# Batch 0 of an attention and mixer kernel: keys ahead of queries, U and V loaded later, the shifted keys in two steps

## The chip, the cores and the metric

The kernel runs on one core of one Trainium2 chip. The metric is the device time of one execution in microseconds (us). Before the change three runs gave 224.07, 226.14 and 224.56 us, a median of 224.56.

Five engines work side by side, each through its own list of instructions in order: PE (TensorE, matrix products), DVE (VectorE), ACT (ScalarE), POOL (GpSimd) and SP (SyncE, which here only issues DMAs). An instruction waits on semaphores that other engines or DMAs raise. Data go from DRAM to the on-chip buffer by DMA; SP and POOL each issue DMAs into a queue of their own. Matrix products are written into eight PSUM banks.

## The reference, cut to what matters

The kernel computes an attention with a local window and a few global keys, and on its output a low-rank token mixer followed by two large products:

```python
# q, k, v: (4 batches, 8 heads, 768 positions, 64), 8 global keys, window of 96
scores = 1/sqrt(64) * q @ k.T                     # per batch and head
keep = (pos_k < 8) | ((0 <= pos_q - pos_k) & (pos_q - pos_k < 96))
scores += -slope[h] * dist                        # dist 96 for far global keys
a = softmax(where(keep, scores, -1e9))
x = (a @ v), heads side by side                   # (4, 768, 512)
h = x.T @ U @ V                                   # U (768, 32), V (32, 768)
u = x + h.T
out = u + relu(u @ w_ch1) @ w_ch2                 # w_ch1 (512, 2048), w_ch2 (2048, 512)
```

## The kernel before

**Tiles.** Two heads make a pair; a batch has four pairs, so there are 16, numbered 0 to 15. A position block has 128 rows, six to a sequence. For each pair the kernel loads q, k and v (384 KB each, `load_one` L94, `load_v` L120, all on SP), casts them to 16 bits (`cast_one` through the helper at L107 and L109, `cast_v` L127), turns q and k on PE so that the head dimension lies on the partitions (`st_tp`, L240), copies the turned tiles out of PSUM (`st_tq`, `st_tk`: qT, kT), and makes kA, a copy of the keys in which the first eight columns of each block are the global keys (`st_K`, L257 and L258). Scores are computed for 11 blocks of 128 by 128 per head: six on the diagonal with kT, five below it with kA.

**Batch 0** (pairs 0 to 3) is handled by steps of its own. The bias is added by PE (L322) before the score products (L329); ACT takes the exponential straight from PSUM (`st_ex`, L349). `st_av` multiplies with the values (L395 with vA, L399 with v; vA is made by `st_A` on POOL, L290, and patched by `st_P` on DVE, L294). `st_norm` divides (L412 to L419), `st_x16` casts to 16 bits (POOL, L423). Then `st_up` multiplies with U (L429), `st_tc` copies the small result, `st_M2` multiplies with V and adds x by an identity product (L487, L492), and `st_ut` copies the sum into uT. The product with w_ch1 (`up_mm`, L535) reads uT and w1. Pairs 4 to 15 (`pair`) take a slower form, in which DVE adds the bias, and are threaded between the big products of earlier batches; the uT of batches 1 to 3 is made by a DMA transposition (`st_X`, L508).

**Before the steps** the kernel issues the first five loads (q and k of pairs 0 and 1, v of pair 0), builds the bias table, sets u16 and v16w to zero on POOL (L190), loads U and V into them (L191, L192), and zeroes two small tiles (L207). `st_first` treats pair 0: turns q, runs two filler products (`warm`, L152), turns k, then copies qT in halves on ACT (L275) and kT and kA in halves on DVE (L276 to L282).

**What sets the order.** A planner in the kernel's own Python writes the instructions out in a fixed order. Each piece of work is a `Step` with an engine, an estimated cost, steps it depends on, and a function that emits it. `clock` holds the planned time of each engine, and "bus" the planned time of the loads. `drain` emits the step that can start first, after adding its `lazy` time, so a step with a hold is passed by others. `HOLD` adds to `lazy` by name, `ONLY` fixes the engine where a step has several `ways`, `SHIFT` moves a step in the order of batch 0, `BEGIN` says when pairs 4 to 7 may begin. Loads have an order (`LOADS`), and each early load waits for the one before it to have been planned. Where PE has no work between 8 and 30 us of planned time, the planner puts filler products (`fill`, L157) on a zero tile.

**Weights.** POOL issues w1 in three DMAs (`load_w1`, L220: the first half in one, then two quarters) and w2 in four (L223).

Of the kernel before, what the change touches and what calls it, by code (L numbers as in the profile page):

```python
# [12 lines left out]
FP16 = mybir.dt.float16  # L13
# [7 lines left out]
def kernel(  # L21
# [115 lines left out]
    ordered = ExitStack()  # L137
    ordered.enter_context(tc.manual_schedule())
    for i in range(2):
        for j in range(2):  # L140
            load_one(i, j)
    load_v(0)

# [43 lines left out]
    u16 = cst.tile([P, NSB, P], FP16, name="u16")  # L187
    v16w = cst.tile([P, S], FP16, name="v16w")
    for t in (u16.rearrange("p n c -> p (n c)"), v16w):
        nc.gpsimd.memset(t.bitcast(I32), 0)  # L190
    nc.gpsimd.dma_start(u16[:, :, 0:R], moe_U.rearrange("(c p) r -> p c r", p=P))  # L191
    nc.gpsimd.dma_start(v16w[0:R], moe_V)  # L192
    ident16 = cst.tile([P, P], FP16, name="ident16")
    nc.vector.tensor_copy(ident16, ident)

# [54 lines left out]
    def st_tk(i, eng):  # L250
        kts[i] = kp.tile([P, S], FP16, name="kT", tag="kT")
        copy(eng, kts[i].rearrange("d (p n) -> d p n", n=NSB), turned[i][1])

    def st_K(i, eng):
        kT = kts[i]
        kA = kp.tile([P, NSB - 1, P], FP16, name="kA", tag="kA")
        eng.tensor_copy(kA.rearrange("d n p -> d (n p)"), kT[:, 0:S - P])  # L257
        eng.tensor_copy(  # L258
            kA[:, 1:, 0:NG], kT[:, 0:NG].unsqueeze(1).broadcast_to((P, NSB - 2, NG))
        )  # L260
        kas[i] = kA

    def st_first(i):
        for j in range(2):
            st_tp(i, j)
            if j == 0:
                warm(2, 448)
        kT = kp.tile([P, S], FP16, name="kT", tag="kT")
        kA = kp.tile([P, NSB - 1, P], FP16, name="kA", tag="kA")
        qT = kp.tile([P, S], FP16, name="qT", tag="qT")  # L270
        tq, tk = turned[i]
        qts[i], kts[i], kas[i] = qT, kT, kA
        for a in range(2):
            ts, ps = slice(a * GT, (a + 1) * GT), slice(a * P // 2, (a + 1) * P // 2)
            nc.scalar.copy(qT[:, ts].rearrange("d (p n) -> d p n", n=NSB), tq[:, ps])  # L275
            nc.vector.tensor_copy(kT[:, ts].rearrange("d (p n) -> d p n", n=NSB), tk[:, ps])  # L276
            ns = slice(0, 2) if a == 0 else slice(2, NSB - 1)
            nc.vector.tensor_copy(
                kA[:, ns].rearrange("d n p -> d (n p)"), kT[:, ns.start * P:ns.stop * P]
            )  # L280
# [137 lines left out]
            return  # L418
        nc.vector.tensor_tensor(xo, ob[:, :, 0:D], rb, ALU.mult)  # L419

    def st_x16(i, hi):
        xo, x16 = heads(i, hi)
        nc.gpsimd.tensor_copy(x16, xo)  # L423

    def st_up(i):
        b, dc = i // NP, i % NP
# [213 lines left out]


    new_batch(0)
    for j in range(2):
# [14 lines left out]
    class Step:  # L658
# [25 lines left out]
        def emit(self, s=None):  # L684
# [8 lines left out]
            if self.move is not None:  # L693
                clock["bus"] = max(clock["bus"], s + self.cost + 1.4) + self.move
                self.end = clock["bus"] + self.tail

    def other(*a, **k):
        waiting.append(Step(*a, **k))
        return waiting[-1]
# [9 lines left out]
    def put(step, frees=()):  # L709
# [11 lines left out]
        assert not granted  # L721

    HOLD = {
# [6 lines left out]
    }  # L730
    ONLY = {
        ('tk', 1): 'DVE', ('tc', 1): 'DVE',
    }
    SHIFT = {
        ('av', 2, 1): -6, ('up', 1): 12, ('ua', 2, 2): -3,
    }
    def add(name, eng, cost, fn, deps=(), **k):
        st = Step(eng, cost, fn, deps, **k)
        if len(name) > 1 and name[1] < NP:
            st.slot = LEVEL.index(name[0]) - 99 + 1.0 * name[1]  # L740
            st.keep = True
            st.slot += SHIFT.get(name, 0)
        st.lazy += HOLD.get(name, 0)
        if name in ONLY:
            st.ways = [w for w in st.ways if w[0] == ONLY[name]]
        steps[name] = st
        (pe_todo if eng == "PE" else waiting).append(st)
        return st

    LEVEL = ["lq", "lv", "w1", "w2", "cq", "tpq", "tpk", "tq", "tk", "ka", "sc", "ex", "cv", "va", "vp",  # L750
             "av", "n", "x16", "up", "tc", "m2", "ut", "ua", "ub", "ur"]

    def landed(name, end):
# [12 lines left out]
        return BEGIN.get(i, 69 + 11.2 * (i - NPE))  # L766

    holder, serial = [], [0]
    for end in (6.6, 7.9, 0, 0, 0, 0, 0, 6.9):
        holder.append(Step("PE", 0, None))  # L770
        holder[-1].end = end
    for n, end in ((("lq", 1, 0), 6.5), (("lq", 1, 1), 8.3), (("lv", 0), 9.9)):
        landed(n, end)
    last_load = [steps["lv", 0]]

    def load(name):
        kind, i = name[:2]
        early = i < NPE
        at = 0 if early else pace(i) - (18 if kind == "lq" else 15)
        if kind == "lq":  # L780
            st = add(name, "SP", 0.5, lambda: load_one(*name[1:]), [("cq", i - 2, name[2])],
                     move=1.2 if early else 1.9, at=at, prev=last_load[0], lazy=0 if early else 1)
        elif kind == "lv":
            st = add(name, "SP", 0.5, lambda: load_v(i), [("cv", i - 2)], move=1.7 if early else 1.9, at=at,
                     prev=last_load[0], lazy=0 if early else 1)
# [10 lines left out]
    LOADS = [  # L796
# [20 lines left out]
    def turns(i):  # L817
# [25 lines left out]
    def first(i):  # L843
# [3 lines left out]
        values(i)  # L847
        for c in range(3):
            sc = add(("sc", i, c), "PE", 0.85 if c < 2 else 0.7, lambda c=c: st_sc(i, c),
                     [], banks=2, at=0 if i or not c else 7.9,  # L850
                     soft=[(("tq", i), 0.4), (("tk", i), 0.4), (("ka", i), 0.6)])
            free_of[sc] = [
                add(("ex", i, c, hi), "ACT", 0.56 if c < 2 else 0.46,
                    lambda c=c, hi=hi: st_ex(i, c, hi), [("sc", i, c), ("av", i - 2, hi)])
                for hi in range(2)
            ]
        for hi in range(2):
            a = add(("av", i, hi), "PE", 0.33, lambda hi=hi: st_av(i, hi),
                    [("ex", i, c, hi) for c in range(3)] + [("va", i), ("vp", i)], banks=1)
            free_of[a] = [add(("n", i, hi), "DVE", 0.75, lambda hi=hi: st_norm(i, hi), [("av", i, hi)])]  # L860
            if i < NP - 1:
                add(("x16", i, hi), "POOL", 0.52, lambda hi=hi: st_x16(i, hi), [("n", i, hi)])
# [310 lines left out]
```

## Time and profile before

| | |
|---|---|
| median of the three runs | 224.56 us |
| the profiled execution | 223.73 us |
| its span, first to last instruction | 221.9 us |
| mean granted TensorE clock | 0.999 |
| PE busy | 216.5 us, 98% of the span |
| DVE, ACT, POOL busy | 156.1, 113.8, 85.6 us |

The profile's page gives the busy time of each engine, slices of the span, and groups of instructions. A group line reads: source line, engine, operation, output <- input, shape, count, then busy time and mean duration. A timeline row reads: start in us, duration in us, engine, line, operation and, in brackets, how long the engine was idle before it and what ended that. L535 is line 535 of the kernel before. "PE busy" counts filler products too, since they are products like any other.

### The profile page before, as it was taken

The numbers are of one execution on the slowest core, as the hardware profiler recorded it, in microseconds if no ns is written. First come the engines' busy times: TensorE is split into PE (matmuls) and PEld (weight loads), VectorE is DVE, ScalarE is ACT, GpSimd is POOL, SyncE is SP. The second block draws the span as 40 slices with busy tenths as digits, with TensorE's granted clock in tenths as the row PEclk, the third lists the DMA queues.
The fourth block names the chain that finished last, engine by engine and source line by source line (L and its number), as shares of the span: only waits on it lengthen the run. The fifth ranks groups of instructions, "written<-read, shape, count | busy, mean of one in ns | idle before, by whom it ended". The sixth has DMA issues, their size and how long they took to land.

```text
span 221.9 us, 5300 instructions
## 1 busy us (share of the span) xinstructions
PE 216.5 (98%) x2103; PEld 142.0 (64%) x2103; DVE 156.1 (70%) x348; ACT 113.8 (51%) x201; POOL 85.6 (39%) x127
## 2 busy tenths in 40 slices
PE   7989999999999999999999999999999999999994
PEld 3555766666555556665665555556998765588883
DVE  5659947564888788769788899789897522084662
ACT  5677766876454207962673407777720044744100
POOL 6477894343823750474536372462410000000000
PEclk9999999999999999999999999999999999999999
DMA  6999999999979999999999889921304112000204
GB/s 190 300 302 201 286 241 196 236 247 208 171 166 248 193 210 167 268 169 243 269 157 240 168 211 242 167 49 35 28 11 130 53 45 94 3 0 0 97 24 165
DMA packets 88871, 35.69 MB, mean 161 GB/s; under 512 B 78320, under 2 KB 85520, under 8 KB 88848
## 3 DMA queue, kind: packets, MB, share of 16 engines
q1 hardware_dynamic: 84320, 31.07, 61.8%
q0 software_dynamic: 4528, 4.29, 12.1%
q8 instruction: 16, 0.26, 0.5%
q14 instruction: 7, 0.06, 0.1%
HBM read 27.46 MB, written 6.29 MB: 152 GB/s over the span
## 4 chain that ended last, share of the span: by engine, by line
PE 91%; DMA 5%; ACT 1%; DVE 1%; issue 0%; SPq 0%; DVEq 0%; ACTq 0%
PE bank L535 37%; PE bank L554 19%; PE bank L621 17%; PE bank L365 4%; DMA qst<-in_q_dram 3%; PE bank L399 3%; PE bank L395 2%; PE bank L460 2%; PE bank L240 2%; DMA kst<-in_k_dram 2%; PE bank L322 1%; PE bank L329 1%; PE bank L437 1%; PE bank L429 1%; ACT ep L384 1%; PE bank L492 1%
## 5 line engine op out<-in xcount | busy, mean ns | idle before, releaser
L535 PE MATMUL bank<-uT,w 128*128 128x384 f16 (+2 forms) x512 | 91.9, 326 | 0.0
L542 ACT ACTIVATE htr<-bank 128x384 f16<-128x384 f32 (+2 forms) x128 | 59.4, 493 | 59.1 <-PE bank L535 58.0
L535 PEld LDWEIGHTS <-w 128*128 128x128 f16 x512 | 47.9, 98 | 28.2
L376 DVE SCALAR_TENSOR_TENSOR sp<-bank,relcat 128x512 f32<-128x512 f32 (+1 forms) x72 | 41.4, 638 | 7.1 <-PE bank L365 7.1
L554 PE MATMUL bank<-w,htr 128*128 128x512 f16 x192 | 46.0, 379 | 0.0
L384 ACT ACTIVATE ep<-sp 128x1408 f16<-128x1408 f32 x24 | 33.0, 1374 | 21.8 <-DVE sp L376 20.7
L423 POOL CAST x<-x_sb 128x384 f16<-128x384 f32 x30 | 18.0, 601 | 31.3 <-DVE x_sb L419 30.3
L554 PEld LDWEIGHTS <-htr 128*128 128x128 f16 x192 | 17.3, 98 | 17.6
L515 POOL CAST x<-x_sb 128x768 f16<-128x768 f32 x11 | 9.5, 866 | 22.8 <-DVE x_sb L470 19.2
L419 DVE TENSOR_TENSOR x_sb<-bank,rcp 128x384 f32<-128x384 f32 x30 | 16.7, 558 | 1.0
L127 POOL CAST v<-vst 128x768 f16<-128x768 f32 x16 | 13.5, 844 | 8.6 <-DMA vst<-in_v_dram 8.6
L399 PE MATMUL bank<-v,ep 128*128 128x65 f16 x192 | 15.8, 194 | 0.2 <-ACT htr L542 0.2
L621 PEld LDWEIGHTS <-htr 128*128 128x128 f16 x144 | 14.1, 98 | 2.1
L399 PEld LDWEIGHTS <-ep 128*128 128x128 f16 x192 | 13.6, 98 | 2.3
L395 PE MATMUL bank<-vA,ep 128*128 128x65 f16 x160 | 13.9, 194 | 0.0
L470 DVE TENSOR_TENSOR x_sb<-bank,x_sb 128x384 f32<-128x384 f32 x24 | 12.3, 548 | 1.7 <-ACT htr L542 1.1
L349 ACT ACTIVATE ep<-bank 128x512 f16<-128x512 f32 (+1 forms) x24 | 11.5, 571 | 2.6 <-PE bank L329 2.6
L109 POOL CAST k<-kst 128x768 f16<-128x768 f32 x12 | 10.8, 898 | 4.1 <-DMA kst<-in_k_dram 3.0
L290 POOL COPY vA<-v 128x650 f16<-128x650 f16 x16 | 12.0, 749 | 0.9
L395 PEld LDWEIGHTS <-ep 128*128 128x128 f16 x160 | 11.0, 97 | 1.8 <-issue 0.2
L621 PE MATMUL bank<-w,htr 128*128 128x256 f16 x96 | 12.0, 273 | 0.0
L639 DVE TENSOR_TENSOR vst<-bank,x_sb 128x256 f32<-128x256 f32 x12 | 5.1, 425 | 9.1 <-PE bank L621 9.1
(112 smaller groups left out, 288.3 us busy)
## 6 DMA issues: line engine op xcount, KB each, us to landing
qst<-in_q_dram SPq DMA_DIRECT2D x16, 384.0 KB, 5.6
kst<-in_k_dram SPq DMA_DIRECT2D x16, 384.0 KB, 5.5
vst<-in_v_dram SPq DMA_DIRECT2D x16, 384.0 KB, 5.3
out_dram<-osb SPq DMA_DIRECT2D x17, 256.0 KB, 2.6
w<-in_moe_w_ch_dram POOLq DMA_DIRECT2D x6, 512.0 KB, 11.5
out_dram<-vst SPq DMA_DIRECT2D x5, 256.0 KB, 2.0
w<-in_moe_w_ch_dram POOLq DMA_DIRECT2D x1, 1024.0 KB, 12.0
out_dram<-osb SPq DMA_DIRECT2D x2, 128.0 KB, 1.7
```

The costliest lines, as they stand in the source:

```text
L127: nc.gpsimd.tensor_copy(vt.rearrange("p n h d -> p h n d")[:, :, :, 0:D], vsts.pop(i).rearrange("p (h n) d -> p h n d", h=2),)
L376: nc.vector.scalar_tensor_tensor(out=sps[i, hi][:, c0:c0 + tot], in0=raw.pop((i, hi, c))[:, 0:tot], scalar=qk_scale / slope[2 * (i % NP) + ...
L384: nc.scalar.activation(ep, sps.pop((i, hi)), AF.Exp, scale=slope[2 * (i % NP) + hi])
L395: nc.tensor.matmul(ob[:, qi], ep[:, OF[qi - 1]:OF[qi - 1] + P], vA[:, qi - 1, hi], start=True, stop=False,)
L399: nc.tensor.matmul(ob[:, qi], ep[:, DG[qi]:DG[qi] + P], vt[:, qi, hi], start=(qi == 0), stop=True,)
L419: nc.vector.tensor_tensor(xo, ob[:, :, 0:D], rb, ALU.mult)
L423: nc.gpsimd.tensor_copy(x16, xo)
L470: nc.vector.tensor_tensor(dst, ups3.pop((i, g))[:, 0:GT].rearrange("p (t d) -> p t d", t=NTG), dst, ALU.add)
L535: nc.tensor.matmul(hps[:, 0:cols], w1_16[:, dc, jt * P:(jt + 1) * P], uTs[b][:, dc, c0:c0 + cols], start=(dc == 0), stop=(dc == NDC - 1),)
L542: nc.scalar.activation(htrs[b, g][:, jt], hps_t.pop((b, g, jt))[:, 0:TG[b][g] * P], AF.Relu)
L554: nc.tensor.matmul(cps, htr[:, jc, ts], w2_16[:, jc], start=(b > 0 and jc == 0), stop=(jc == NJC - 1),)
L621: nc.tensor.matmul(accs[b, n, acc], x[:, c], y[:, c], start=(fresh and c == 0), stop=(c == HC - 1), skip_group_check=not fresh,)
```

## The change

Eight things are edited.

1. The loads, casts and turns of pairs 0 and 1 take k before q, and so do the loads of pairs 2 and 3. In `st_first`, the filler between the two turns is seven products of 128 columns instead of two of 448.
2. u16 and v16w are set to zero on DVE. The two small tiles are set to zero inside `finish_table`, which runs after batch 0.
3. The loads of U and V become a step, `load_uv`, on POOL, with its place in `LOADS` behind v of pair 2; the product with U depends on it.
4. In batch 0, `st_K` is split into `st_ka` (the copy of 640 columns, on DVE) and `st_kg` (the global keys, on DVE; on ACT for pair 1).
5. The planner's starting clocks, the planned durations of the loads and some planned start times are changed.
6. Another table of holds: `HOLD` now names batch 0 alone and holds w1's first load by 0.4; `SHIFT` and `ONLY` are others.
7. Pair 5 may begin at 40 instead of 44.
8. The differences of w2's parts that DVE forms for later batches (`w_sum`) are planned at 98 + 8 times their number instead of from 95 on.

Since the planner orders everything by its clocks, the order of instructions changes on all engines, not only in the lines that are edited.

```diff
-        for j in range(2):
+        for j in (1, 0):
             load_one(i, j)
 ...
     for t in (u16.rearrange("p n c -> p (n c)"), v16w):
-        nc.gpsimd.memset(t.bitcast(I32), 0)
-    nc.gpsimd.dma_start(u16[:, :, 0:R], moe_U.rearrange("(c p) r -> p c r", p=P))
-    nc.gpsimd.dma_start(v16w[0:R], moe_V)
+        nc.vector.memset(t.bitcast(I32), 0)
 ...
     lows = [cst.tile([P, P], FP16, name=f"low{j}") for j in range(2)]
-    for t in lows:
-        nc.gpsimd.memset(t, 0.0)
+
+    def load_uv():
+        nc.gpsimd.dma_start(u16[:, :, 0:R], moe_U.rearrange("(c p) r -> p c r", p=P))
+        nc.gpsimd.dma_start(v16w[0:R], moe_V)
 
     def finish_table():
+        for t in lows:
+            nc.gpsimd.memset(t, 0.0)
         nc.gpsimd.tensor_copy(relcat, wide)
 ...
+    def st_ka(i, eng):
+        kA = kp.tile([P, S], FP16, name="kA", tag="kA")
 ...
+            eng.tensor_copy(kA[:, 0:S - P], kts[i][:, 0:S - P])
+        kas[i] = kA[:, 0:S - P].rearrange("d (n p) -> d n p", p=P)
+
+    def st_kg(i, eng):
+        kA = kas[i]
+        copy(eng, kA[:, 1:, 0:NG], kA[:, 0, 0:NG].unsqueeze(1).broadcast_to((P, NSB - 2, NG)))
 ...
     def st_first(i):
-        for j in range(2):
+        for j in (1, 0):
             st_tp(i, j)
-            if j == 0:
-                warm(2, 448)
+            if j:
+                warm(7, P)
 ...
-    clock = {"PE": 6.9, "ACT": 6.5, "DVE": 8.3, "POOL": 5.6, "SP": 4.0, "bus": 9.9}
+    clock = {"PE": 6.5, "ACT": 6.9, "DVE": 7.6, "POOL": 5.6, "SP": 4.0, "bus": 10.0}
 ...
     HOLD = {
-        ('ex', 0, 2, 0): 0.2, ('n', 0, 0): 0.4, ('tk', 3): 0.2, ('cv', 0): 0.8, ('n', 1, 1): -0.3,
-        ('n', 2, 1): -0.3, ('ex', 2, 0, 0): 0.2, ('ex', 3, 2, 1): 0.2, ('xt', 5): -1, ('half', 7, 1): -2,
-        ('x16', 5, 0): -2, ('xt', 7): -2, ('w2', 3): -0.5, ('e', 6, 1): 0.8, ('cx', 6): 0.8,
 ...
+        ('w1', 0): 0.4, ('ut', 0, 0): -0.6, ('tc', 1): -0.3, ('va', 2): 0.2, ('ex', 2, 1, 0): 0.2,
+        ('tc', 2): -0.3, ('w1', 2): 0.8, ('ut', 2, 1): 0.8, ('cv', 0): 0.2,
     }
     ONLY = {
-        ('tk', 1): 'DVE', ('tc', 1): 'DVE',
+        ('kg', 1): 'ACT',
     }
     SHIFT = {
-        ('av', 2, 1): -6, ('up', 1): 12, ('ua', 2, 2): -3,
+        ('av', 2, 1): 1.5, ('sc', 3, 1): 12, ('sc', 3, 2): -6, ('sc', 1, 2): 12, ('tpq', 2): 12,
+        ('av', 0, 1): -1.5,
     }
 ...
-    BEGIN = {NP: 31, NP + 1: 44, NP + 2: 50, NP + 3: 58}
+    BEGIN = {NP: 31, NP + 1: 40, NP + 2: 50, NP + 3: 58}
 ...
+        elif kind == "uv":
+            st = add(name, "POOL", 1.5, load_uv, move=1.0, prev=last_load[0])
 ...
-        ("lq", 2, 0), ("lq", 2, 1), ("lv", 1), ("lq", 3, 0), ("lq", 3, 1), ("lv", 2), ("lv", 3),
+        ("lq", 2, 1), ("lq", 2, 0), ("lv", 1), ("lq", 3, 1), ("lq", 3, 0), ("lv", 2), ("uv", 0), ("lv", 3),
 ...
-        if i < NP + 1:
+        if i < NP:
+            ka = add(("ka", i), (("DVE", 0.34), ("ACT", 0.7)), 0, lambda e: st_ka(i, e),
+                     [("tpk", i)] + old if ONLY.get(("ka", i)) == "ACT" else [("tk", i)])
+            add(("kg", i), (("DVE", 0.2), ("ACT", 0.24)), 0, lambda e: st_kg(i, e), [("ka", i)])
 ...
+        elif i < NP + 1:
             add(("ka", i), "DVE", 0.7, lambda: st_K(i, nc.vector), [("tk", i)])
 ...
-        u = add(("up", i), "PE", 0.34, lambda: st_up(i), [("x16", i, 0), ("x16", i, 1)], banks=1)
+        u = add(("up", i), "PE", 0.34, lambda: st_up(i), [("x16", i, 0), ("x16", i, 1), ("uv", 0)], banks=1)
 ...
-                wsums[k, part] = other("DVE", 0.7, lambda k=k, part=part: w_sum(k, part), deps, at=95, lazy=0.8 if k < 2 else 0.4)
+                wsums[k, part] = other("DVE", 0.7, lambda k=k, part=part: w_sum(k, part), deps, at=98 + 8 * (2 * k + part), lazy=0 if k < 2 else 0)
```

More of the change, by code (lines that the diff above doesn't have):

```diff
@@ L252, in st_tk @@
         copy(eng, kts[i].rearrange("d (p n) -> d p n", n=NSB), turned[i][1])
+    def st_ka(i, eng):
+        kA = kp.tile([P, S], FP16, name="kA", tag="kA")
+        if eng is nc.scalar:
+            m = -(-(S - P) // NSB)
+            nc.scalar.copy(kA[:, 0:m * NSB].rearrange("d (p n) -> d p n", n=NSB), turned[i][1][:, 0:m])
+        else:
+            eng.tensor_copy(kA[:, 0:S - P], kts[i][:, 0:S - P])
[3 more added lines that the diff above has]
+        copy(eng, kA[:, 1:, 0:NG], kA[:, 0, 0:NG].unsqueeze(1).broadcast_to((P, NSB - 2, NG)))
     def st_K(i, eng):
@@ L419, in st_norm, with st_x16 @@
         nc.vector.tensor_tensor(xo, ob[:, :, 0:D], rb, ALU.mult)
-    def st_x16(i, hi):
+    def st_x16(i, hi, eng=nc.gpsimd):
         xo, x16 = heads(i, hi)
-        nc.gpsimd.tensor_copy(x16, xo)
+        copy(eng, x16, xo)
     def st_up(i):
@@ L642 @@
     new_batch(0)
-    for j in range(2):
+    for j in (1, 0):
         cast_one(0, j, nc.vector)
@@ L695, in emit, with end @@
                 self.end = clock["bus"] + self.tail
+    class Both(tuple):
+        rank, keep, first = 0, True, None
+        @property
+        def end(self):
+            ends = [w.end for w in self]
+            return None if None in ends else max(ends)
     def other(*a, **k):
@@ L745, in add @@
             st.ways = [w for w in st.ways if w[0] == ONLY[name]]
+        if name[0] in ("ka", "kg", "x16") and name not in ONLY:
+            st.ways = st.ways[:1]
         steps[name] = st
@@ L748, in add @@
         return st
-    LEVEL = ["lq", "lv", "w1", "w2", "cq", "tpq", "tpk", "tq", "tk", "ka", "sc", "ex", "cv", "va", "vp",
+    LEVEL = ["lq", "lv", "w1", "w2", "uv", "cq", "tpq", "tpk", "tq", "tk", "ka", "kg", "sc", "ex", "cv", "va", "vp",
              "av", "n", "x16", "up", "tc", "m2", "ut", "ua", "ub", "ur"]
@@ L768 @@
     holder, serial = [], [0]
-    for end in (6.6, 7.9, 0, 0, 0, 0, 0, 6.9):
+    for end in (7.2, 7.0, 0, 0, 0, 0, 0, 6.9):
         holder.append(Step("PE", 0, None))
         holder[-1].end = end
-    for n, end in ((("lq", 1, 0), 6.5), (("lq", 1, 1), 8.3), (("lv", 0), 9.9)):
+    for n, end in ((("lq", 1, 1), 7.5), (("lq", 1, 0), 8.5), (("lv", 0), 9.9)):
         landed(n, end)
@@ L781, in load @@
             st = add(name, "SP", 0.5, lambda: load_one(*name[1:]), [("cq", i - 2, name[2])],
-                     move=1.2 if early else 1.9, at=at, prev=last_load[0], lazy=0 if early else 1)
+                     move=1.1 if early else 1.9, at=at, prev=last_load[0], lazy=0 if early else 1)
         elif kind == "lv":
-            st = add(name, "SP", 0.5, lambda: load_v(i), [("cv", i - 2)], move=1.7 if early else 1.9, at=at,
+            st = add(name, "SP", 0.5, lambda: load_v(i), [("cv", i - 2)], move=1.45 if early else 1.9, at=at,
                      prev=last_load[0], lazy=0 if early else 1)
@@ L831, in turns @@
         ]
-        if i < NP + 1:
+        if i < NP:
+            ka = add(("ka", i), (("DVE", 0.34), ("ACT", 0.7)), 0, lambda e: st_ka(i, e),
+                     [("tpk", i)] + old if ONLY.get(("ka", i)) == "ACT" else [("tk", i)])
+            add(("kg", i), (("DVE", 0.2), ("ACT", 0.24)), 0, lambda e: st_kg(i, e), [("ka", i)])
+            if ONLY.get(("ka", i)) == "ACT":
+                free_of[tp[1]] = [Both((steps["tk", i], ka))]
+        elif i < NP + 1:
             add(("ka", i), "DVE", 0.7, lambda: st_K(i, nc.vector), [("tk", i)])
@@ L849, in first @@
             sc = add(("sc", i, c), "PE", 0.85 if c < 2 else 0.7, lambda c=c: st_sc(i, c),
-                     [], banks=2, at=0 if i or not c else 7.9,
-                     soft=[(("tq", i), 0.4), (("tk", i), 0.4), (("ka", i), 0.6)])
+                     [], banks=2, at=0 if i or not c else 7.3,
+                     soft=[(("tq", i), 0.4), (("tk", i), 0.4), (("ka", i), 0.4), (("kg", i), 0.6)])
             free_of[sc] = [
@@ L861, in first @@
             if i < NP - 1:
-                add(("x16", i, hi), "POOL", 0.52, lambda hi=hi: st_x16(i, hi), [("n", i, hi)])
+                add(("x16", i, hi), (("POOL", 0.52), ("ACT", 0.5)), 0,
+                    lambda e, hi=hi: st_x16(i, hi, e), [("n", i, hi)])
             else:
                 steps["x16", i, hi] = steps["n", i, hi]
-        u = add(("up", i), "PE", 0.34, lambda: st_up(i), [("x16", i, 0), ("x16", i, 1)], banks=1)
+        u = add(("up", i), "PE", 0.34, lambda: st_up(i), [("x16", i, 0), ("x16", i, 1), ("uv", 0)], banks=1)
         free_of[u] = [add(("tc", i), (("DVE", 0.29), ("ACT", 0.3)), 0, lambda e: st_tc(i, e), [("up", i)])]
```

3 rows, old and new, of the table HOLD are left out of this document.

## The prediction

> **What bounds the kernel now.** I read the page first, then the engines in stretches of 10 us, then PE, POOL and the DMA queues of the first 30 us. PE (TensorE) is busy 98% of the span. In the stretches, mean columns left out here are of no use; what counts is the second number, PE's busy time.
>
> ```profile
> PE 216.5 (98%) x2103; PEld 142.0 (64%) x2103; DVE 156.1 (70%) x348; ACT 113.8 (51%) x201; POOL 85.6 (39%) x127
> ```
> ```profile
> 0.00:10.00 10.00, 8.74 (x55) 3.77 (x55) 6.09 (x19) 5.98 (x14) 5.62 (x17) 1.00 0.90 235
> 10.00:20.00 10.00, 9.30 (x132) 5.76 (x132) 6.76 (x15) 7.81 (x16) 6.81 (x9) 1.00 1.10 270
> 20.00:30.00 10.00, 9.88 (x163) 7.27 (x163) 8.41 (x21) 6.64 (x17) 8.82 (x15) 1.00 1.08 259
> 30.00:40.00 10.00, 10.00 (x92) 6.42 (x90) 6.63 (x12) 7.23 (x15) 5.46 (x8) 1.00 1.19 210
> ```
>
> From 30 us on PE has no hole to speak of up to the last output; before that it has 1.26 + 0.70 + 0.12 us of idle time, and inside "busy" 22 filler matmuls (L157), which compute nothing. So the change, which rebuilds batch 0, can only move the moment at which the dense stretch begins. That moment is the first matmul with w1 (L535). In the timeline it starts at 28.41 us:
>
> ```profile
> 10.56 1.65 PE L157 MATMUL bank<-x 128*128 128x128 f16 x18
> 12.91 0.51 PE L240 MATMUL bank<-ident,q 128*128 128x128 f16 x6 [0.70 <-ACT q L107]
> ...
> 28.41 0.98 PE L535 MATMUL bank<-uT,w 128*128 128x384 f16 x5
> ```
>
> What it needs from outside is the first half of w1. POOL's timeline and the DMA issues between 7 and 18 us show when that leaves and lands (the last column is us from issue to landing):
>
> ```profile
> 15.89 0.79 POOL L220 DMA_DIRECT2D w<-in_moe_w_ch_dram  x1
> 16.68 1.04 POOL L109 CAST k<-kst 128x768 f16<-128x768 f32 x1
> 18.19 0.84 POOL L127 CAST v<-vst 128x768 f16<-128x768 f32 x1 [0.48 <-DMA vst<-in_v_dram]
> ```
> ```profile
> w<-in_moe_w_ch_dram POOLq DMA_DIRECT2D x1, 1024.0 KB, 12.0
> ```
>
> 15.89 + 12.0 = 27.9 us: only 0.5 us before PE uses it. PE's own chain and this load are almost level, so I follow both.
>
> **PE's own chain.** (1) *Zeros of u16 and v16w.* Off POOL go 0.82 + 0.41 us (L190), onto DVE come two memsets, each some 0.4 us by L147's 0.27 for 256 columns. DVE's wait of 1.07 us before its first cast hides them; if it did not, 0.3 us would reach the first cast. The casts that ran beside the POOL memsets took 0.83 and 0.81 us, the later ones 0.55, so the second may end 0.26 earlier. (2) *Keys first.* Before, the second cast (5.89) feeds the turned keys (to 6.82), DVE copies half of kT (to 7.42), and the first score matmul follows at 7.62; DVE then holds the second half up to 8.84 while PE waits 0.2. After, DVE's six copies for kT and kA run while the queries are cast and turned, and ACT's two copies (0.48 each) come last. Gain 0.26 + 0.2, and 0.1 for the shorter last copy: about 0.5. (3) *Pair 1.* DVE alone copied qT (0.96), kT (0.95), kA (0.33 + 0.17), one after the other, to 12.81. Now ACT takes qT and the global keys, and the scores of pair 1 no longer stand behind pair 2's turned queries, which waited 0.70 (the row above). That wait goes, and the 0.29 at 21.6 probably too. The key casts of pairs 2 and 3 leave POOL (0.83, 1.04) for DVE (0.55 each), one query cast goes from ACT to DVE and one the other way. DVE was busy 4.67 of 5 us from 17 to 22; if it becomes late there, 0.5 of the gain is lost. ACT's copy of the global keys has no row; between 0.17 (DVE's) and 0.48, and as the small ACT copies took 0.27 I take that. It stands on ACT before four exps that PE does not await at once. (4) *Filler.* In the built order 34 blocks of 128 filler columns become 35: no gain. Sum: -0.5 - 0.7 - 0.3 = -1.5 us, bounds -2.2 and -0.5. One more thing moves: ahead of the first w1 matmul the old order has all of batch 0 but one M2 block (two L487 and six L492, 0.66 us), the new one all but that and one product with U (six L429, 0.33). So PE would stand ready for w1 at 28.41 - 1.5 - 0.33 = 26.6 us.
>
> **U and V.** Their issues (1.04 + 0.53) leave POOL's head and follow vA of pair 0 (ended 11.96): 13.5, before v of pair 1 lands (14.3), so they are hidden there. U then lands some 6.1 later, at 18, and V before it; the product with U starts no earlier than 21: hidden. If SP's loads pass ahead, q and k of pair 2 gain at most 0.6 (v's cast at 10.33 to q's at 12.02 is 1.7, two neighbouring loads elsewhere 1.14), and v of pair 2 loses most of it again.
>
> **The load of w1.** In the built order its issue no longer stands behind vA of pair 1 but behind the cast of v of pair 2. Queued on POOL ahead of it are now also two x16 casts, which end at about 17, before v of pair 2 is there. That v lands after the same bytes as before, at 18.14 (18.19 in POOL's row), bounds 17.5 and 18.2. Cast 0.84: w1 is issued at 18.9 (18.4 to 19.05) instead of 15.89, 3.0 us later. How long does it then take? The DMA queues (packets on each) from 19.4 to 21.0, when POOL's queue had the engines to itself, and from 22.0 to 24.5, when q and k of pair 4 moved too:
>
> ```profile
> q0 software_dynamic: 134, 0.27, 100.5%
> q1 hardware_dynamic: 1, 0.00, 0.3%
> ```
> ```profile
> q0 software_dynamic: 176, 0.36, 76.5%
> q1 hardware_dynamic: 172, 0.26, 33.5%
> ```
>
> 134 packets in 1.6 us is 84 per us; shared it is 70. The load has 512 packets of 2 KB (1024 KB). Its first ones moved 1.8 us after the issue began. Alone: 1.8 + 6.1 = 7.9 us; shared throughout: 1.8 + 7.3 = 9.1; measured with stragglers: 12.0. After the change it does not meet the loads of v of pair 2, but those of pairs 4 and 5, issued earlier. I take the middle of 9.1 and 12.0, 10.5. Landing: 18.9 + 10.5 = 29.4; bounds 18.4 + 7.9 = 26.3 and 19.05 + 12.0 = 31.05.
>
> [...]
>
> **The later stages.** The two memsets of the lows (0.36 together) go to 28 us on POOL, ahead of the table that DVE reads at 36.9: hidden by 6 us. The holds for pairs 4 to 7 are gone. The tightest place they touched: the last transposition of batch 1's uT is issued at 80.83, lands 2.7 later at 83.5, and the fourth matmul of the batch, which reads it, starts at 83.40 + 3 x 0.16 = 83.9. A slack of 0.35 without its two holds of 2 us: I count +0.3, bounds 0 and 1.2 (one transposition issue). Sums of w2 move later on DVE by up to 27 us, their products come after 150: nothing.
>
> **Sum.** The w1 load ends last: 29.45 - 28.41 = +1.04; PE's work that now stands behind it +0.33; the transposition +0.3: **+1.7 us**. The profiled execution took 223.73 us (span 221.9), so 225.4; the three runs have a median of 224.56, 0.83 above it, and on that the forecast is **226.2 us**.
>
> **Rivals.** *The load is in time.* If w1 lands by 26.6 (7.7 us after the issue, just below "alone"), PE's chain decides: -1.5 + 0.3 = -1.2, 223.4. For it: the load is then away from v of pair 2. Against: no POOL load in the trace was that quick; the fastest of half the size took 8.7. *It only shares, with no stragglers.* At 70 packets per us all the way it lands at 28.0: -0.4 + 0.33 + 0.3 = +0.2, 224.8. Against: 28 of the 512 packets came only between 25.5 and 28 us. *The load keeps its 12.0 us.* Then it lands at 31.0: +2.6 + 0.33 + 0.3 = +3.2, 227.8. For it: that is the only duration measured at this size, and four more SP loads are free to run against it. *The early gain is not there,* because q and k of pairs 2 and 3 are late or DVE is full: with w1 binding it changes nothing until PE is 2.8 us later than I have it, so it gives 226.2 too. *More goes than I can see:* a start 2.2 us faster with the load in time, 222.4 or less.
>
> **How the numbers follow.** This kernel's runs tell a change of about 1% (2.2 us) from none. Forecast, w1 landing between 28.5 and 30.1: 0.40, 225.3 to 226.9. Sharing alone: 0.15, 224.3 to 225.3. Load late, 226.9 and above: 0.28. Load in time: 0.12, 222.6 to 224.3. More: 0.05. The range reaches from the in-time case to beyond the late one: 222.9 to 228.0. Faster by over 1%: 0.07 (the last case and the lower edge of the in-time one); slower by over 1%: 0.31 (the late case and the upper edge of the forecast); within 1%: 0.62.
>
> **What would show it.** Right: the scores of pair 1 start near 11 us instead of 13.26; POOL issues w1 near 18.9; PE idles 2 to 3 us ahead of its first w1 matmul, which starts at 29 to 30, with no idle 0.7 at 12. Wrong: a first w1 matmul before 28 without idle time ahead of it (the load in time), or new waits after 40 us over 0.5 in sum (the holds mattered more), or PE late for batch 0 by its own chain.

## The result, and the profile after

| | before | after |
|---|---|---|
| median of six runs each, same chip | 224.25 us (224.07 to 226.14) | 227.75 us (226.40 to 228.92) |
| ratio after / before | | 1.0145, 95% interval 1.0114 to 1.0176 |
| profiled execution | 223.73 us | 226.40 us |
| its span | 221.9 us | 224.6 us |
| PE ready for w1 (its last product before, by start and pitch) | 28.41 us | 26.8 us |
| first w1 product | 28.41 us | 29.75 us |
| from there to the start of the last product | 190.15 us | 191.47 us |

The change made the kernel slower by 1.45%. The ratios in this document leave out executions that are more than 1.5% above the fastest of the same kernel (in e8 below that leaves three of ten), so where the granted clock is the point I give medians over all executions and say how many had which clock.

Busy time of the engines of the changed kernel, and then the same stretches of 10 us as in the prediction (columns: length, then busy time of PE, weight loads, DVE, ACT, POOL, granted clock, DMA share, GB/s):

```profile
PE 216.3 (96%) x2101; PEld 141.2 (63%) x2104; DVE 157.5 (70%) x349; ACT 115.6 (51%) x205; POOL 80.6 (36%) x122
```
```profile
0.00:10.00 10.00, 8.46 (x73) 4.26 (x74) 6.71 (x22) 6.38 (x15) 3.12 (x11) 1.00 0.83 247
10.00:20.00 10.00, 9.69 (x131) 5.64 (x132) 9.45 (x18) 8.89 (x18) 7.84 (x11) 1.00 1.18 298
20.00:30.00 10.00, 7.17 (x128) 5.38 (x128) 5.97 (x15) 5.99 (x15) 9.02 (x16) 1.00 1.11 239
30.00:40.00 10.00, 9.79 (x94) 6.27 (x93) 3.86 (x9) 6.15 (x13) 5.43 (x7) 1.00 1.21 217
```

PE's total is the same 216 us. The second row is fuller than before (9.69 against 9.30), the third emptier (7.17 against 9.88): batch 0 runs earlier, and then PE stands still. PE's timeline shows where:

```profile
11.02 0.23 PE L344 MATMUL bank<-qT,kT 64*128 64x128 f16 x2
12.43 0.51 PE L242 MATMUL bank<-ident,k 128*128 128x128 f16 x6
...
26.64 0.33 PE L507 MATMUL bank<-ident,x 128*128 128x128 f16 x3
29.75 0.34 PE L550 MATMUL bank<-uT,w 128*128 128x384 f16 x1 [2.78 <-DMA w<-in_moe_w_ch_dram]
```

The score products of pair 1 start at 11.02 instead of 13.78 (with their bias, at 10.71 instead of 13.26), and the turns that follow them have no wait of 0.70. Three products of 128 columns from 26.64 on are the last work that PE has. By their starts and pitch PE is free at 26.64 + 3 x 0.056 = 26.8; the row's 2.78 us of waiting for w1 counts from the end of the last of them, a little later. The chain of the changed kernel between 18 and 33 us, in order of time (start, length, what it was), names the cause from end to end:

```profile
18.24 0.78 POOL v L127
19.02 10.69 DMA w<-in_moe_w_ch_dram
29.70 0.05 issue
29.75 0.34 PE bank L550
30.09 0.35 PE bank L444 x6
30.44 0.03 issue
30.46 0.02 DVEq L109
30.48 0.45 issue
30.93 0.30 DVE tmp L109
31.24 0.05 issue
31.28 0.34 PE bank L502
```

Read it downwards. POOL casts v of pair 2, then issues w1 (3.13 us later than the 15.89 of before), the load takes 10.69 us, PE starts at once. The lower half is a second, smaller loss: the six products with U of pair 3 (L444) now stand behind the first w1 product, so they wait with it; DVE copies their result at 30.93, and the product with V (L502) cannot start before 31.28. PE has only four more w1 products to put in between, and by starts and pitch a gap of 0.38 us is left.

The span grew by 2.7 us: 1.34 at the first w1 product, 1.32 behind it. The six runs differ from their profile more than before's do: 227.75 is 1.35 above 226.40, while 224.25 is 0.52 above 223.73. The granted clock was 1.0 in the profiled execution; the other five had 0.992, 0.990, 0.992, 0.992 and 0.985. So there were three things to explain: the start, the later microsecond, and the clock.

### The profile page after: what moved, and what is told of

Read it like the earlier page. It is cut to its first block, busy times and chain, and to the rows that moved or that the text cites. A ratio compares the mean times of both kernels' runs of the same rounds, so it can differ in the third digit from the quotient of the medians.

```text
span 224.6 us, 5298 instructions
## 1 busy us (share of the span) xinstructions
PE 216.3 (96%) x2101; PEld 141.2 (63%) x2104; DVE 157.5 (70%) x349; ACT 115.6 (51%) x205; POOL 80.6 (36%) x122
## 4 chain that ended last, share of the span: by engine, by line
PE 75%; DMA 11%; DVE 9%; issue 1%; POOL 1%; SPq 1%; POOLq 0%; DVEq 0%
PE bank L550 31%; PE bank L569 18%; PE bank L636 16%; DMA w<-in_moe_w_ch_dram 5%; DMA qst<-in_q_dram 3%; PE bank L380 3%; DMA kst<-in_k_dram 2%; DMA kT<-k 2%; PE bank L414 2%; PE bank L475 2%; DVE sp L391 2%; PE bank L410 1%; DVE htr L594 1%; PE bank L242 1%; DVE x_sb L485 1%
## 5 line engine op out<-in xcount | busy, mean ns | idle before, releaser
L109 POOL CAST x<-x_sb 128x384 f16<-128x384 f32 x30 | 16.8, 562 | 46.9 <-DVE x_sb L434 46.7
L410 PEld LDWEIGHTS <-ep 128*128 128x128 f16 x160 | 10.9, 97 | 1.7
L654 DVE TENSOR_TENSOR osb<-bank,osb 128x256 f32<-128x256 f32 x12 | 5.1, 423 | 8.5 <-PE bank L636 8.4
## 6 DMA issues: line engine op xcount, KB each, us to landing
w<-in_moe_w_ch_dram POOLq DMA_DIRECT2D x6, 512.0 KB, 10.7
w<-in_moe_w_ch_dram POOLq DMA_DIRECT2D x1, 1024.0 KB, 10.7
```

The costliest lines, as they stand in the source:

```text
L109: eng.tensor_copy(dst, src)
L410: nc.tensor.matmul(ob[:, qi], ep[:, OF[qi - 1]:OF[qi - 1] + P], vA[:, qi - 1, hi], start=True, stop=False,)
```

## The experiments

The theories. **A**: the landing of w1's first half sets the start, and its issue behind v of pair 2 sets the landing. **B**: the loss lies in the later stages. **C**: PE's idle time ahead of the first w1 product also lowers TensorE's clock for a while. **D** came later: the later microsecond is that of the dropped holds for pairs 4 to 7. Line numbers in the variants are a few higher than in the changed kernel.

| run | edit | median, us (executions) | ratio to before | executions with the clock under 0.995 |
|---|---|---|---|---|
| e1_w1_early | after, w1 earlier | 223.54 (10) | 0.9987 (0.9959 to 1.0015) | 0 |
| e2_before_w1_late | before, w1 later | 225.59 (10) | 1.0059 (1.0029 to 1.0090) | 1 |
| e3_w1_split | after, two halves of that load | 224.80 (10) | 0.9986 (0.9946 to 1.0027) | 1 |
| e4_fill_hole | after, 12 filler products | 228.04 (4) | 1.0171 (1.0129 to 1.0213) | 0 |
| e5_after_again | after, unchanged | 227.72 (10) | 1.0124 (1.0085 to 1.0163) | 8 |
| e6_w1_later | after, w1 later still | 230.08 (4) | 1.0246 (1.0153 to 1.0339) | 4 |
| e7_fill_less | after, 5 filler products | 227.28 (4) | 1.0130 (1.0061 to 1.0200) | 0 |
| e8_w1_quarters_early | after, w1 earliest, in quarters | 228.73 (10) | 1.0008 (0.9961 to 1.0055) | 6 |
| e9_late_holds | after, old holds for pairs 4 to 7 | 227.97 (4) | 1.0169 (1.0121 to 1.0216) | 3 |
| e10_early_holds | e1 with these holds | 224.20 (12) | 1.0001 (0.9978 to 1.0024) | 0 |
| e11_early_holds_m2 | e10, one product moved | 224.14 (12) | 0.9990 (0.9969 to 1.0011) | 0 |
| e12_fill_again | e7 once more | 226.40 (6) | 1.0083 (1.0050 to 1.0116) | 1 |

The kernel before had medians of 224.31, 224.07, 224.12 and 224.58 us beside the four groups, and never a clock under 0.998.

### Where w1 is issued: e1 and e2

In e1 only POOL's list changes: w1's issue stands behind vA of pair 1. In e2 the kernel before gets the changed kernel's place for it.

```diff
 # e1, in the changed kernel
     def st_A(i):
...
         vas[i] = vA
+        if i == 1:
+            load_w1(0, 2)
...
-            st = add(name, "POOL", 0.8, lambda: load_w1(i, m), move=2.9 * m, prev=last_load[0])
+            st = add(name, "POOL", 0.8, lambda: load_w1(i, m) if i else None, move=2.9 * m, prev=last_load[0])
```
```diff
 # e2, in the kernel before (the planner's step as in e1)
     def cast_v(i):
...
         vts[i] = vt
+        if i == 2:
+            load_w1(0, 2)
```

> The changed kernel with one instruction moved: POOL issues the first half of w1 directly behind vA of pair 1, as before the change, and not behind the cast of v of pair 2. All else keeps its place. Theory A (the w1 load alone sets the start of the dense stretch): issue at 16.4 us instead of 19.0, landing 10.7 to 12.0 later, at 27.1 to 28.4; PE idles 0.3 to 1.6 us ahead of its first w1 product instead of 2.8; the time falls by 1.3 to 2.4 us. Rival B (the other order of later work and the dropped holds cost it): it moves by less than 0.5 us. Rival C (the wait itself lowers the granted clock, 0.985 to 0.992 in five of six runs of the changed kernel): clock back to 0.999 and another 1.0 to 1.3 us off the median.

> The kernel before with one instruction moved: the first half of w1 is issued behind the cast of v of pair 2. Theory A: issue at 19.0 us, landing 29.7 to 31.0 instead of 27.9; PE waits 1.3 to 2.6 us at its first w1 product; the profiled span grows by as much, to 223.2 to 224.5. Rival B: less than 0.5 us. Rival C: the granted clock of the timed runs falls to about 0.99 as well and the median rises by 1 us more than the span of a run at full clock.

POOL's timeline and PE's of e1, then PE's of e2:

```profile
17.11 0.79 POOL L222 DMA_DIRECT2D w<-in_moe_w_ch_dram  x1
```
```profile
28.02 0.34 PE L552 MATMUL bank<-uT,w 128*128 128x384 f16 x1 [0.54 <-DMA w<-in_moe_w_ch_dram]
```
```profile
29.12 0.99 PE L537 MATMUL bank<-uT,w 128*128 128x384 f16 x5 [0.91 <-DMA w<-in_moe_w_ch_dram]
```

In e1 the issue is 1.9 us earlier, the load takes 10.9 us, and the first w1 product starts at 28.02, 1.73 earlier than in the changed kernel. Its profiled span is 222.5, 2.1 shorter; its median is 4.2 below that of the changed kernel. In e2 the issue comes at 18.54, the load takes 10.5 us, PE waits 0.91 where before it did not wait, and the time rises by 0.6%. The stretch behind the first w1 product is 190.17 us in e2 and 190.15 before: moving the start moves the end by as much. A holds in both directions, in e2 with a shorter wait than the 1.3 to 2.6 us expected, since the issue came 0.5 us before the assumed 19.0 and the load took less than the assumed 10.7 to 12.0. But 4.2 us is twice what the two profiles of e1 and after differ by, which A alone does not give.

### A smaller load: e3

```diff
-            st = add(name, "POOL", 0.8, lambda: load_w1(i, m), move=2.9 * m, prev=last_load[0])
+            st = add(name, "POOL", 0.8, lambda: [load_w1(i + j) for j in range(m)], move=2.9 * m, prev=last_load[0])
```

> The changed kernel, the first half of w1 loaded by two DMAs of a quarter (512 KB) each at the same place on POOL; the first twelve products need the first quarter only. Theory A: the first quarter lands 6.5 to 8 us after the issue at 19.0, at 25.5 to 27.0, so PE no longer waits (0 to 0.3 us); the time falls by 2.5 to 2.8 us; the second quarter lands near 30.5, used after 36. Rival B: less than 0.5 us. Rival C: the clock returns to 0.999 and the median falls by up to 1.3 us more.

The first w1 products need only the first 512 KB. In the profiled execution these were issued late, at 20.22 (v of pair 2 came late), and landed 7.6 us afterwards, at 27.8; PE became ready at 28.5 and started without waiting for w1. The median fell to 224.80, close to the kernel before, with the issue still behind v of pair 2. So it is the landing of those bytes that counts, not the place of the issue as such. The ten executions spread widely, from 222.54 to 227.17; why was not settled.

### The clock: e4 to e7, e9 and e12

e5 is the changed kernel again. e6 issues w1 behind vA of pair 2. e4, e7 and e12 put filler products on a zero tile ahead of the first w1 product (12 in e4, 5 in e7 and e12).

```diff
 # e6: as e1, but
+        if i == 2:
+            load_w1(0, 2)
 # e7, e12 (range(12) in e4), in up_mm
+        if (b, g, jt) == (0, 0, 0) and 0 in dcs:
+            for _ in range(5):
+                nc.tensor.matmul(hps, zw[:, 0:P], zw, start=True, stop=True)
```

> The changed kernel with twelve filler products of 512 columns (2.6 us) in front of the first w1 product, where PE idles for 2.8 us. Theory A without a part for the clock: span and times unchanged within 0.3 us, idle 0.2 us. Rival C (PE's idling lowers the clock or makes PE slower behind it): the granted clock of the timed runs rises to 0.999 and their median falls by 1.0 to 1.3 us, to that of the profiled run.

> The changed kernel, nothing edited. In its profiled execution the granted clock was 1.0 and the time 226.4 us; the five other executions had clocks of 0.985 to 0.992 and 226.86 to 228.92. Theory A (the load of w1 sets the start, the idle time is all that is lost): a median near 226.4, and the low clocks were a matter of that chip. Theory C (PE's idle time ahead of the first w1 product of about 2.8 us also lowers the clock for a while behind it): clocks under 0.995 again in most executions, a median of 227 to 228, and, if the profile falls on such an execution, slices below full clock right behind the hole at 27 to 30 us.

> The changed kernel with the first half of w1 issued behind vA of pair 2 instead of ahead of it, 0.8 us later (that copy's 0.73 to 0.85). Theory A: landing near 30.5, first w1 product 0.8 later, time +0.8 over the unedited kernel beside it, clock as there. Theory C: PE's hole grows from 2.8 to 3.6 us, every execution shows a clock of 0.985 to 0.992, the profile shows the slices behind the hole at less than full clock, and the time is 1.5 to 2.5 above the 226.4 of the full-clock execution.

> The changed kernel with 5 filler products of 512 columns (5 x 0.22 = 1.1 us) ahead of the first w1 product, few enough to end before w1 lands. Theory A: nothing changes but the length of the hole (2.8 to 1.7 us): the same time as the unedited kernel beside it, within 0.4 us. Theory C: clocks of 0.998 to 1.0 in all executions, and a median 0.8 to 1.5 us below the unedited kernel, at 226 to 226.8.

e5 repeats the finding: eight of ten executions at 0.984 to 0.992, a median of 227.72; the two at full clock took 225.35 and 225.71. That is C's side. The profiled execution is one of these two, and its hole was short, since PE itself was late; PE's timeline of e5:

```profile
29.04 0.34 PE L550 MATMUL bank<-uT,w 128*128 128x384 f16 x1 [0.93 <-DMA w<-in_moe_w_ch_dram]
```

In e6 the profiled execution itself had the lower clock. Its first w1 product, and stretches around it (length, PE busy, granted clock, DMA share, GB/s):

```profile
32.27 0.50 PE L552 MATMUL bank<-uT,w 128*128 128x384 f16 x1 [4.50 <-DMA w<-in_moe_w_ch_dram]
```
```profile
30.00:32.00 2.00, 0.00 (x0) 1.00 1.17 193
32.00:34.00 2.00, 1.73 (x10) 0.50 1.22 197
34.00:35.00 1.00, 1.00 (x6) 0.50 1.21 196
35.00:36.00 1.00, 1.00 (x12) 0.80 1.20 194
36.00:38.00 2.00, 2.00 (x18) 1.00 1.22 211
```

All four executions have the lower clock, as C expected; but the hole is 4.50 us and not 3.6, as both v of pair 2 and the load came late, and the median of 230.08 lies above C's price too. After the hole the granted clock is 0.50. What half the clock does to the work can be read from the same four w1 products, first in e6 and then in the profiled execution of the changed kernel, at full clock:

```profile
33.21 1.49 PE L552 MATMUL bank<-uT,w 128*128 128x384 f16 x4
```
```profile
30.26 0.81 PE L550 MATMUL bank<-uT,w 128*128 128x384 f16 x4
```

PE is "busy" in both, 1.49 us against 0.81. In steps of 0.2 us the clock is 0.50 from 32.0 to 35.4, 3.4 us:

```profile
31.80:32.00 0.20, 0.00 (x0) 0.99 1.18 189
32.00:32.20 0.20, 0.00 (x0) 0.50 1.25 202
...
35.20:35.40 0.20, 0.20 (x3) 0.50 1.24 200
35.40:35.60 0.20, 0.20 (x4) 0.98 1.21 196
```

Half speed over 3.4 of some 226 us is a mean clock of 1 - 1.7/226 = 0.992, the number that nine of the 13 executions of the changed kernel with a lower clock show. By the same estimate two such spells would make 0.985, the lowest of after's; no trace shows two. From the first w1 product to 35.4 the spell takes away half of 3.1 us of work, **1.6 us**. The net loss can be smaller: from the first w1 product to the start of the last product e6 takes 192.12 us, 0.7 more than the changed kernel at full clock (191.47), and the gap behind the product with U, for one, is not there in e6. e9 (below) was also caught with it, behind a hole of 2.41 us:

```profile
28.00:30.00 2.00, 0.00 (x0) 1.00 1.10 272
30.00:32.00 2.00, 1.60 (x10) 0.52 1.17 257
32.00:33.00 1.00, 1.00 (x5) 0.50 1.20 205
33.00:34.00 1.00, 1.00 (x10) 0.75 1.23 204
```

Here it lasts from 30.1 to 33.5, again 3.4 us. The length of the hole alone does not decide it: 2.41 us of idle time was enough in e9, while after's own 2.78 us left the clock at 1.0. What else decides it, no run here shows. Behind shorter holes the clock stayed up: the profiled executions have 0.999 behind 0.54 us (e1) and 0.93 us (e5), and 1.0 behind 0.91 us (e2). Of all twenty executions of e1 and e2 one had a lower clock.

The filler runs price it less cleanly. e4 overshoots: PE became ready later than in after's profile, its fillers end at 30.43 while w1 landed at 29.3, and a wait of 1.35 us ahead of 87.77, for a transposed x, came on top. Its clock is full in all four executions, but the time is not the 1.0 to 1.3 lower that C expected. e7 has full clock four times of four, and 227.28 misses the expected 226 to 226.8. Its profiled execution, 228.28, shows a wait that has nothing to do with w1; in its chain from 84 to 102 us (start, length, what):

```profile
89.00 4.05 DMA kst<-in_k_dram
...
94.03 6.58 DMA kT<-k
...
100.63 0.34 DVE kA L272
...
101.16 0.14 DVE tmp L109
```

A transposition of keys took 6.58 us, the copy of kA waited for it on DVE, and behind that, in DVE's list, stood the small copy that PE needed: PE waited 1.87 us. Four executions with such waits among them do not show what the clock was worth; e12 is the same program again.

> The same program as e7_fill_less, timed more often: there the four executions had full clock but 225.73 to 228.28 us, too few to say whether the clock's return is worth anything. Priced by the rows of e6_w1_later and e9_late_holds (half clock for 3 us behind the hole, so 1.5 us of work lost), theory C gives clocks of 0.998 to 1.0 in all executions and a median 1.0 to 1.6 below the changed kernel's 227.7: 226.1 to 226.7. Rival (the lower clock is there, but the time is set by something else, such as w1's landing and the waits behind 85 us): clock 1.0 and a median of 227.2 or more.

226.40 us, inside the expected 226.1 to 226.7; five of six at full clock. The sixth was the profiled one: w1 landed at 31.4 there (issue 19.69, 11.7 us), the hole behind the fillers was 2.56 us, the clock fell to half from 33.2 to 36.6, and that execution took 229.34, the longest. Over e7 and e12 together nine of ten executions have full clock and the median is 226.8; over after and e5, 13 of 16 have the lower clock and the median is 227.7. So C's mechanism holds: filling part of the hole brings the clock back. Its price is less certain. The medians differ by 0.9 us, but the two groups overlap (225.1 to 229.3 and 225.4 to 230.5), and with so few executions, partly on different chips, that difference is not clear of noise. By the traces a spell takes up to 1.6 us of work, and the stretch behind the first w1 product is 0.7 (e6) and 1.3 (e12, 192.76) longer than after's.

### Earliest: e8

```diff
     def cast_v(i):
...
         vts[i] = vt
+        if i == 1:
+            load_w1(0)
...
     def st_A(i):
...
         vas[i] = vA
+        if i == 1:
+            load_w1(1)
```

> The changed kernel with the first half of w1 as two DMAs of 512 KB, the first issued behind the cast of v of pair 1 (near 14.9 us), the second behind vA of pair 1 (near 17). Theory A: the first lands by 25.5, PE does not wait for w1 at all, its first w1 product starts at 27.3 to 27.6, time 222.6 to 223.3 (222.9), below the kernel before by 0.4 to 0.8%. Theory B (the start is not what decides, the later stages give it back): 224 or more. Theory C: as A, clock 1.0.

The step of the planner issues nothing for w1's first half here, as in e1. The first quarter was issued at 14.34, landed at 23.2, and PE's first w1 product came at 27.82 without a wait for w1, as A has it. But the time was not 222.9: 224.56 in the profiled execution, and in six of ten executions the clock was 0.983 to 0.993 and the time 228.4 to 229.9. POOL's timeline shows what was late beside the early load:

```profile
21.82 0.83 POOL L127 CAST v<-vst 128x768 f16<-128x768 f32 x1 [2.30 <-DMA vst<-in_v_dram]
```

v of pair 3, cast at 20.2 in the changed kernel's second profile, is cast 1.6 us later, and PE stands still for 0.8 us in batch 0 ahead of 24.3, waiting for POOL. If the low clock comes from idle time here too, the six executions with it idled longer somewhere; none of them was profiled, so that is open. This expectation failed: issuing the load still earlier did not help.

### The later microsecond: e9, e10, e11

e9 puts back the old table's holds for pairs 4 to 7; e10 does so in e1; e11 moves the product with V of pair 3 behind two more w1 products.

```diff
 # e9, e10, e11
     HOLD = {
+        ('xt', 5): -1, ('half', 7, 1): -2, ('x16', 5, 0): -2, ('xt', 7): -2, ('e', 6, 1): 0.8, ('cx', 6): 0.8,
...
 # e11 as well
     SHIFT = {
...
+        ('m2', 3): 5,
```

> The changed kernel with the old table's holds for pairs 4 to 7 put back (batch 0's holds stay the new ones). From its first w1 product to its last product the changed kernel took 191.5 us, the kernel before 190.15, of which 0.33 is work that moved behind that start; about 1.0 is waits. Theory D (the dropped holds make them): that stretch becomes 190.5 to 190.9, the waits of 0.2 to 0.3 near 85, 99, 130 and 144 us go, the median falls by 0.6 to 1.0 from the 227.7 of the changed kernel. Rival: the waits come from elsewhere (pair 5's earlier begin, DMAs that land late): 191.2 or more, no change of the median beyond 0.3. The hole ahead of w1 and the granted clock stay in both.

> The changed kernel with w1 issued behind vA of pair 1, as in the first run, and with the old holds for pairs 4 to 7. Theory A with D: 222.6 to 223.0 us, 0.6 to 0.8% below the kernel before. Without D: as the first run, 223.5. Clock 0.998 to 1.0 in both.

> As e10_early_holds, and the product with V of pair 3 is moved behind two more w1 products, so that PE does not wait for the copy of the small result of pair 3 (0.4 us at 29.0 in the first run). Expected 0.2 to 0.4 below e10_early_holds, 222.3 to 222.8. If the copy isn't what PE waits for there, the same as e10_early_holds.

D fell. In e9 the stretch behind the first w1 product is 193.29 us; without the 1.6 us of half clock that is 191.7, not 190.5 to 190.9. PE's timeline of e9 also has a wait for POOL that after's has not:

```profile
107.00 0.32 PE L452 MATMUL bank<-u,x 128*128 128x32 f16 x6 [0.64 <-POOL x L109]
```

And it lacks the gap of 0.4 behind the product with U; with both allowed for, e9 and after come to the same 191.1. The median is 227.97. e10 against e1: a stretch of 191.57 against 191.15, and 224.20 against 223.54 us. The holds give nothing that these runs can show, in either kernel. e11 against e10: 190.97 against 191.57, the gap of 0.38 us is gone, as PE's timeline of e11 shows by the row without a bracket and the six w1 products ahead of it:

```profile
27.07 0.34 PE L552 MATMUL bank<-uT,w 128*128 128x384 f16 x1
27.26 0.51 PE L446 MATMUL bank<-x,u 128*128 128x128 f16 x6
27.60 1.14 PE L552 MATMUL bank<-uT,w 128*128 128x384 f16 x6
28.64 0.34 PE L504 MATMUL bank<-v16w,tmp 128*128 128x384 f16 x1
```

So in the profiles 0.4 of the later microsecond is the copy behind the moved product with U. The profiled span of e11, 221.4, is the shortest of all, but its median of 224.14 against e10's 224.20 does not show the 0.2 to 0.4 that I expected. The rest (the stretch less before's 190.15, less 0.33 of moved work, and less the 0.4 where that gap is still there) is 0.6 us in after, 0.7 in e10, 0.3 in e1 and e5, 0.5 in e11: single waits of 0.1 to 0.3 us, whose places change from one execution to the next. No run gave them a cause.

No version beats the kernel before: e1 and e11 are 0.1% below it with intervals that take in 1. Their medians are 4.2 and 3.6 us below the changed kernel's.

## Why the prediction was right or wrong

The forecast of 226.2 was 1.55 below the 227.75 measured; the range of 222.9 to 228.0 held it, with 0.25 to spare. "Within 1%" had 0.62 and "slower" 0.31: the kernel was slower by 1.45%. The likeliest case was the wrong side of the line. That 227.75 is almost the 227.8 of the rival *load late* is luck: that rival has w1 landing at 31.0, and in the profile it landed at 29.7; a lower clock, which no case of the prediction has, filled the difference.

- **What bounds the kernel: right.** PE stays bound, and the start of the w1 products moves the end (e1, e2).
- **PE's own chain, ready at 26.6: right in after's profile,** 26.8, with pair 1's scores at 11.02 and the wait of 0.70 gone. But that was the best of the profiled executions: PE was ready at 27.1 (e11), 27.3 (e1), 27.5 (e10), 28.0 (e5) and 28.5 (e3) in others, against 28.41 before. With 0.33 us of that being moved work, the gain is between none and 1.3 us, so the -1.5 was not reached, and in some executions not the lower bound of 0.5 either. In e5 PE waited 0.70 us at 21.1 for kA on DVE, the lateness of DVE that the prediction had named. The worth of the single parts (zeros, keys first, filler) was not tried by itself.
- **U and V hidden: right.** U was issued at 11.65, V at 12.68, and no product with U waited for them.
- **The issue of w1, 18.9: right,** 19.02; behind v of pair 2, as said.
- **The load, 10.5 us: right,** 10.7; the landing, 29.4 forecast, came at 29.7. The 10.5 was the middle of two bounds and not a mechanism, and other executions had 10.1 to 11.7 at about the same place, so some of the closeness is luck.
- **The moved product with U, +0.33: incomplete.** I counted the product's own 0.33 us, and not that its result is copied before PE can go on: 0.4 more (e11).
- **Later stages, +0.3 by the transposition: mis-sized.** The waits were 1.0 us in after's profile: the 0.4 above, 0.2 ahead of 85.8, at the fourth product that reads the transposed uT, as I had named it, and some more. The holds that I blamed were not the cause: with them put back, PE still idles at that place (0.06 us in e10 and e9 by the busy time of short slices, 0.07 in after).
- **The profile and the median.** In terms of the profiled execution I had 225.4, and it took 226.40; of this 1.0 the landing is 0.3 and these waits are 0.7. To come from there to the median I took over the 0.83 us of before, and it was 1.35: the other 0.5 of the miss. That step failed: behind a hole in PE that I forecast myself, at 2 to 3 us, I priced nothing for the clock. In 13 of 16 executions of the changed kernel the mean clock was 0.984 to 0.992. No profile fell on one of them; in the three profiles that caught the lower clock, of e6, e9 and e12, it was half clock for 3.4 us behind such a hole, up to 1.6 us of work. The kernel before has no such hole (0.70 us is the longest between its products) and no mean clock under 0.998.
- **The rivals.** *Load in time* and *sharing only* (9.1 us by the packets) fell: the first half, loaded whole, took 10.1 to 12.0 us in every profile here, wherever it was issued. In after's trace POOL's queue moved 96 packets up to 23 and then, to 28, 73 to 85 per us beside SP's 71 to 87; that makes at most some 490 of the load's 512 by 28.0, and it landed at 29.7. What makes the tail is open: the next quarter of w1, issued at 24.55, was in the same queue by then, so some of the 490 may be its. *Load late* would have landed at 31.0; e12's profiled execution is that case (11.7 us, 31.4). *Early gain missing* changes nothing while w1 binds, as said: e5's PE was 1.2 us later than after's and its span still shorter, since w1 landed at 29.0. It even left a shorter hole, 0.93 us, and full clock: here an earlier PE only waits longer. Of the issues on POOL, w1's took 0.79 us at its new place as at its old one, with no cast from an fp32 tile on DVE beside it in after's profile. U's issue took 1.03 us at its new place and 1.04 at its old one, with a cast of keys on DVE beside it in both; V's took 0.65 instead of 0.53.

## What to carry to other kernels

Where a load decides when a dense stretch begins, read its issue in the queue that carries it: here the load took 10 to 12 us wherever it stood, an issue 1.9 us earlier moved the start by 1.7 and the median by 4.2, and splitting off the part that is needed first moved the median by 2.9, with a wide spread. A wait that you forecast for TensorE can cost more than its length: behind 2.4 us and more there came 3.4 us of half clock in three of four profiles, and in 13 of 16 executions of the changed kernel the mean clock was lower, so price that before calling the change neutral. And when a product slips behind a waiting one, follow its result through the copy to the next product, not the product's own time alone.

## What was not expected of the hardware

- TensorE's granted clock fell to 0.50 for 3.4 us behind idle times of 4.50, 2.41 and 2.56 us (e6, e9, e12), and stayed at 1.0 behind 2.78 us (after). It began between 0.3 us before work resumed (e6, e9) and 1.8 us after it (e12: work from 31.4, half clock from 33.2).
- The mean clock is a quick test for it in this kernel: the profiles with one spell have 0.992 or 0.993, those without have 0.998 to 1.0. By the estimate 1 - 2 x (3.4/2)/226, 0.985 would be two; none was profiled.
- The load of 1024 KB took 10.1 to 12.0 us in the traces of before and after and of all the variants that keep it whole; its halves of 512 KB took 7.6 to 11.0 (e3, e8). When it began as early as 14.34, v of pair 3 was cast 1.6 us later (e8).
- The transposition of one pair's keys by DMA took 6.58 us once (e7), where the median of the three in that stretch was 4.4.
